# V loads on GpSimd's queue and an earlier trigger for K loads in a batched decode attention kernel

## The chip, the cores and the metric

The kernel runs on 1 core of a Trainium2 chip. The metric is the device time of one execution in microseconds. A profile of one execution goes with each version: its times run from the first to the last instruction (the span). The engines are TensorE (PE), VectorE (DVE), ScalarE (ACT), GpSimd (POOL) and SyncE (SP). Each runs its own instruction stream in order and waits on semaphores; SyncE only issues DMAs here.

## The reference

Eight sequences each decode one token. x is 8 x 1 x 640, and K and V caches are 8 x 32 heads x 4096 keys x 128, all in bf16. The output is the sum of x, an attention block and an MLP block, both on the normalized x:

```python
def _A_ref(x, k_cache, v_cache, wq, wo):
    q = (x @ wq).reshape(B, Sq, Hq, Dh).transpose(0, 2, 1, 3)
    scores = jnp.einsum("bhqd,bhkd->bhqk", q, k) * (Dh ** -0.5)
    p = _softmax(scores, axis=-1)
    o = jnp.einsum("bhqk,bhkd->bhqd", p, v)
    return o.transpose(0, 2, 1, 3).reshape(B, Sq, Hq * Dh) @ wo

def _B_ref(x, w1, b1, w2, b2):
    y = _layernorm(x, axis=-1)
    return _gelu(y @ w1 + b1) @ w2 + b2

xn = _layernorm(x, axis=-1)
return x + _A_ref(xn, ...) + _B_ref(xn, ...)
```

Every head has its own K and V, read once. They are 537 MB of the 552 MB that the kernel reads.

## The kernel before, in words

The work is cut into NQ = 32 pairs; pair i is one sequence with 8 heads. Its K is one load of 128 partitions x 256 keys x 128 (8.389 MB, 64 KB per partition), its V another of the same size. On chip there are three slots of that size: KA for the K of even pairs, KB for that of odd pairs, and VS for every V. So K(i) can be loaded once the K of pair i-2 is used up, and V(i) once the V of pair i-1 is.

A pair goes through these steps, named as in the code:

- `qrep(i)` (GpSimd) repeats the pair's queries, `pe_qbc(i)` and `act_qbc(i)` (TensorE, ScalarE) spread them over the partitions into `qbc_sb`.
- `k_ready(i)` (GpSimd) waits for K(i) and sets a small tile, on which TensorE's work of the pair waits.
- The scores of 80 of the 256 keys in each partition are made on TensorE: `pe_T` turns K tiles (transposes, the last of them is `kt`), `act_T` copies them from PSUM, `pe_QK` multiplies. Those of the other 176 keys are made on VectorE in three chunks (`dve_chunk`: multiply by `qbc_sb`, add halves, reduce); the end of the last chunk is `km`. `dve_sel` brings TensorE's scores in before the third chunk.
- `dve_max(i)` makes the maximum (`nb`), and `act_exp(i)` takes the exps of 8 heads; it waits for `nb` of its pair and for the PV of the pair before, since P_sb has one buffer.
- `pe_PV(i)` multiplies the 256 blocks of V by the exps, once V(i) and the exps are there; `act_O` copies the result out, and `o_norm` (GpSimd) scales it.

TensorE runs the scores of pair i+1 before PV(i). After the last pair come the MLP and the output projection with wo; their weights are loaded into slots that have come free (w1 and w2 into KA after pair 30, wo into KB after pair 31). V(30) is loaded in two parts.

The order on each engine is fixed by hand: each step is entered with a position, all are sorted by it, and each engine replays its calls in that order. With o = 100 i: `load_k(i)` stands at o - 51, `qrep(i)` at o - 52, `act_qbc(i)` at o - 10.5, `k_ready(i)` at o - 2, `load_v(i)` at o + 50, `act_exp(i)` at o + 90, `pe_PV(i)` at o + 150, `act_O(i)` at o + 171, `o_norm(i)` at o + 175. A waiting instruction holds up all that follows on its engine. In the kernel before, SyncE issues all K and V loads, in turn, and all land in one hardware queue. `KLATE = 6`: the first K loads wait for `kt` and `km` of pair i-2, those from pair 6 on for its exps. All operations are recorded through one helper, so the profile shows line 111 for nearly all of them.

Of the kernel before, what the change touches and what calls it, by code (L numbers as in the profile page):

```python
# [192 lines left out]
def bass_parallel_sum__gqa_block_cached__mixer_channel_mlp__decode_kernel(  # L193
# [34 lines left out]
    TPB = 8  # L228
    NS = 2
    LOOP0, LOOPN = 2, 15  # L230
    KLATE = 6
    assert NKEY == 256 and NQ == 32
    SLOT = NKEY * DH
    KA, KB, VS = 0, 1, 2
# [4 lines left out]
    V_CUT = (0, 192, 256)  # L239
# [4 lines left out]
    def chunks(i):  # L244
        jd = NKEY - jp_of(i)
        n = 3
        return [(jd * c // n, jd * (c + 1) // n) for c in range(n)]

    def kslot(i):
        return KA if i % 2 == 0 else KB  # L250
# [8 lines left out]
    with ExitStack() as es:  # L259
        sb = lambda name, shape, dt: es.enter_context(nc.sbuf_tensor(name, shape, dt))  # L260
        ps = lambda name, shape, dt: es.enter_context(nc.psum_tensor(name, shape, dt))
        sem = lambda name: es.enter_context(nc.semaphore(name))

        S_sb = sb("S_sb", [P, 3, SLOT], BF)
        tile = [S_sb[:, s, :].rearrange("p (j d) -> p j d", d=DH) for s in range(3)]
# [6 lines left out]
        def scratch(n, rows=P, slot=KB):  # L272
# [71 lines left out]
        pe, dve, act, sp, pool = (_Eng(sem(f"{n}_s")) for n in ("pe", "dve", "act", "sp", "pool"))  # L344
        pe2, act2, fin, fin2 = (_Eng(sem(n)) for n in ("pe2_s", "act2_s", "fin_s", "fin2_s"))
        ld_s = [_Dma(sem(f"ld_s{s}")) for s in range(3)]
        ld_x, ld_b1, ld_b2, ld_wq, ld_w1, ld_w2a, ld_w2b, st_a, st_o = (
            _Dma(sem(n)) for n in ("ld_x", "ld_b1", "ld_b2", "ld_wq", "ld_w1", "ld_w2a", "ld_w2b", "st_a", "st_o"))
        ld_vl = [_Dma(sem(f"ld_vl{q}")) for q in range(1, len(V_CUT) - 1)]
        ld_wl = [_Dma(sem(f"ld_wl{q}")) for q in range(2)]  # L350
        ld_wn = [_Dma(sem(f"ld_wn{q}")) for q in range(len(WN_CUT) - 1)]
        tk = {}
# [8 lines left out]
        def cache_src(cache, i):  # L361
            hq, b = divmod(i, B)
            return cache[b, hq * HS:(hq + 1) * HS].rearrange("h (p j) d -> (h p) j d", j=NKEY)

        def load_k(i):
            s = kslot(i)
            if i >= KLATE:
                sp.wait(tk[("exp", i - 2)])
            elif i >= 2:
                sp.wait(tk[("kt", i - 2)], tk[("km", i - 2)])  # L370
            elif s == KB:
                sp.wait(tk["qmm"])
            tk[("k", i)] = ld_s[s].sig(sp.dma_start(tile[s], cache_src(A_k_cache, i)))
# [4 lines left out]
            load("w2a", ld_w2a, w2_sb, B_w2[0:FB * P, :].rearrange("(p c) n -> p c n", c=FB))  # L378

        def load_v(i):  # L380
            sp.wait(tk["qmm"] if i == 0 else tk[("pv", i - 1)])
            if i != NQ - 2:
                tk[("v", i)] = [ld_s[VS].sig(sp.dma_start(tile[VS], cache_src(A_v_cache, i)))]
                return
            tk[("v", i)] = []
            for d, lo, hi in zip([ld_s[VS]] + ld_vl, V_CUT[:-1], V_CUT[1:]):
                if lo:
                    d.n += 1
                tk[("v", i)].append(
                    d.sig(sp.dma_start(tile[VS][:, lo:hi, :], cache_src(A_v_cache, i)[:, lo:hi, :])))  # L390

        def load_b1():
            act.wait(tk[("kt", NQ - 2)], tk[("km", NQ - 2)])
# [226 lines left out]
        def dve_chunk(i, c):  # L620
            s = i % 2
            lo, hi = chunks(i)[c]
            w = hi - lo
            kt = tile[kslot(i)][:, lo:hi, :]
            dve.wait(tk[("k", i)], tk[("qb", i)])
            t = dve.sig(dve.tensor_tensor(
                kt, kt, qbc_sb[:, s, :][:, None, :].to_broadcast([P, w, DH]), ALU.mult))
            tk[("ym", i)] = t
            dve.wait(t)
            t = dve.sig(dve.tensor_tensor(kt[:, :, 0:DH // 2], kt[:, :, 0:DH // 2], kt[:, :, DH // 2:DH], ALU.add))  # L630
            dve.wait(t, tk.get(("exp", i - 2)))
            tk[("km", i)] = dve.sig(dve.tensor_reduce(Sd_sb[:, s, lo:hi], kt[:, :, 0:DH // 2], AX.X, ALU.add))
# [179 lines left out]
        at(NQ * Q - 55, load_mlp)  # L812
        at(NQ * Q - 54.9, load_w2b)
        at(-870, load_k, 0)
        at(NQ * Q - 60.1, zero_w2b)
        at(-800, consts_pool)
# [17 lines left out]
        for i in range(NQ):  # L834
            o = i * Q
            last = i == NQ - 1
            if i:
                at(o - 51, load_k, i)
            at(o + 50, load_v, i)
            at(o - 52, qrep, i)  # L840
            at(o - 2, k_ready, i)
            at(o - 11, pe_qbc, i)
            at(o - 10.5, act_qbc, i)
            nt = jp_of(i) // TPB
            w = 42.0 / nt
            for t in range(nt):
                at(o + w * t, pe_T, i, t)
                at(o + w * (t + 0.4), act_T, i, t)
                at(o + w * (t + 1.5), pe_QK, i, t)
            at(o + 2, dve_chunk, i, 0)  # L850
            at(o + 26, dve_chunk, i, 1)
            at(o + 52, dve_sel, i, 0)
            at(o + 55, dve_sel, i, 1)
            at(o + 58, dve_chunk, i, 2)
            at(o + 84, dve_max, i)
            at(o + 90 if i else o + Q + 45, act_exp, i)
            at(o + Q + 48, pe_RS, i)
            at(o + Q + 57, dve_rinv, i)
            at(o + Q + 50, pe_PV, i)
            if not last:  # L860
                at(o + Q + 71, act_O, i)
            at(o + Q + 75, o_norm, i)
# [81 lines left out]
```

## Time and profile before

| | |
|---|---|
| time, median of 3 runs | 1281.4 us (1281.25 to 1281.62) |
| span of the profiled execution | 1280.1 us |
| read from HBM | 551.80 MB, 431 GB/s over the span |
| share of the 16 DMA engines' time in SyncE's queue | 99.7% |
| VectorE busy | 1101.6 us, 86% |
| TensorE busy | 672.0 us, 52% |
| ScalarE busy | 477.0 us, 37% |
| GpSimd busy | 109.3 us, 9% |
| mean granted TensorE clock | 0.564 |

The rows of the timeline give a start, a duration, an engine, the operation with its output and inputs, and in brackets how long the engine had stood idle and what ended that. "SPq" and "ACTq" are DMA issues: they show when a load was handed to a queue, not when it moved. In the list of issues the last number is the median time from issue to landing.

### The profile page before, as it was taken

Reading aid. Unit: us, or ns where it says so; the run is one execution under the profiler, and the core shown is the slowest. Engines: PE = TensorE matmul, PEld = TensorE weight load, DVE = VectorE, ACT = ScalarE, POOL = GpSimd, SP = SyncE. Lnnn points to the kernel's source line nnn. Section 1 sums busy time; section 2 is a strip of 40 time slices with the busy share of each in tenths; the row PEclk is TensorE's granted clock in tenths of the full one; section 3 lists DMA queues with packets and bytes.
Section 4 is the critical chain, followed back from the end, with each engine's and each line's share of the span. In section 5 each row is a group of like instructions: output and inputs, shape, how many; then the busy total and the mean of one; then the engine's idle time right before and its main releaser. Section 6 shows DMA issues by size and latency. Waiting matters only on the chain.

```text
span 1280.1 us, 34355 instructions
## 1 busy us (share of the span) xinstructions
PE 672.0 (52%) x13906; PEld 573.2 (45%) x13906; DVE 1101.6 (86%) x681; ACT 477.0 (37%) x906; POOL 109.3 (9%) x119
## 2 busy tenths in 40 slices
PE   1636555446645446545456554456454466464476
PEld 1435444335535345444345444345343355353465
DVE  1899999889888889888898888898888898888894
ACT  0524444233444233443234443234442334442331
POOL 0020010000000000000000000000000000000050
PEclk9755565565565556555555555556555656655665
DMA  9999999999999999999999999999999999999998
GB/s 419 427 433 431 432 430 432 442 432 430 430 442 428 432 432 436 436 430 432 432 442 430 430 432 438 432 430 434 436 436 430 432 430 442 432 428 434 432 440 367
DMA packets 10785, 551.99 MB, mean 431 GB/s; under 512 B 1242, under 2 KB 1523, under 8 KB 1812
## 3 DMA queue, kind: packets, MB, share of 16 engines
q1 hardware_dynamic: 10736, 551.79, 99.7%
q8 instruction: 9, 0.15, 0.0%
q10 hardware_dynamic: 36, 0.02, 0.0%
q14 instruction: 4, 0.03, 0.0%
HBM read 551.80 MB, written 0.01 MB: 431 GB/s over the span
## 4 chain that ended last, share of the span: by engine, by line
DMA 47%; DVE 37%; issue 11%; ACT 4%; DVEq 0%; SPq 0%; PE 0%
DMA S_sb<-in_A_k_cache_dram 45%; DVE S_sb L111 26%; DVE Sd_sb L111 8%; ACT P_sb L111 4%; DMA S_sb<-in_A_wo_dram 2%; DVE S_ps L111 1%; DVE mx_sb L111 1%; DVE mbT_sb L111 0%; DVE mxT_sb L111 0%; DVE ri_sb L111 0%; DVE NB_sb L111 0%; DVEq L109 0%; DVE mq_sb L111 0%; DVE mb_sb L111 0%; SPq L111 0%
## 5 line engine op out<-in xcount | busy, mean ns | idle before, releaser
L111 PE MATMUL TR_ps<-ident_bf,S_sb 128*128 128x128 bf16 (+1 forms) x2570 | 343.3, 280 | 353.5 <-POOL kr_sb L111 333.2
L111 DVE TENSOR_TENSOR S_sb<-S_sb,qbc_sb 128x7552 bf16<-128x7552 bf16 (+1 forms) x96 | 388.7, 4049 | 128.3 <-DMA S_sb<-in_A_k_cache_dram 128.0
L111 PEld LDWEIGHTS TR_ps<-ident_bf,S_sb 128*128 (+2 forms) x2570 | 245.7, 103 | 411.7 <-issue 338.5
L111 DVE TENSOR_REDUCE Sd_sb<-S_sb 128x59 f32<-128x3776 bf16 (+1 forms) x96 | 390.2, 4065 | 6.0
L111 ACT ACTIVATE KT_sb<-TR_ps 128x1024 bf16<-128x1024 bf16 x320 | 327.0, 1024 | 121.6 <-PE TR_ps L111 109.6
L111 PE MATMUL PV_ps<-P_sb,S_sb 128*128 128x8 bf16 x8192 | 224.0, 175 | 140.6 <-DMA S_sb<-in_A_v_cache_dram 137.9
L111 PEld LDWEIGHTS PV_ps<-P_sb,S_sb 128*128 128x128 bf16 x8192 | 221.3, 103 | 143.3 <-DMA S_sb<-in_A_v_cache_dram 140.5
L111 DVE TENSOR_TENSOR S_sb<-S_sb 128x3776 bf16<-128x3776 bf16 (+1 forms) x96 | 206.5, 2151 | 3.3
L111 ACT ACTIVATE P_sb<-Sd_sb,NB_sb 128x256 bf16<-128x256 f32 x256 | 126.3, 494 | 210.9 <-DVE NB_sb L111 210.9
L111 PE MATMUL S_ps<-qrep_sb,KT_sb 128*128 128x8 bf16 x2560 | 121.9, 177 | 50.9 <-ACT KT_sb L111 47.8
L111 ACT ACTIVATE oU_sb<-PV_ps 128x8 f32<-128x8 f32 x31 | 5.5, 178 | 375.8 <-PE PV_ps L111 375.8
L111 PEld LDWEIGHTS S_ps<-qrep_sb,KT_sb 128*128 128x128 bf16 x2560 | 91.7, 103 | 82.4 <-ACT KT_sb L111 41.1
L111 POOL TENSOR_TENSOR oT_sb<-oU_sb,ri_sb 128x8 bf16<-128x8 f32 x31 | 71.8, 2315 | 370.8 <-DVE S_sb L111 315.3
L111 POOL COPY qrep_sb<-qT_sb 128x128 bf16<-128x128 bf16 x32 | 18.3, 573 | 474.7 <-PE S_ps L111 455.1
L111 ACT ACTIVATION_READ_ACCUMULATOR P_sb<-Sd_sb,NB_sb 128x1 f32 x256 | 47.8, 187 | 0.0
L111 DVE TENSOR_TENSOR S_ps<-S_ps,mask_sb 128x320 f32<-128x320 f32 (+1 forms) x65 | 31.6, 486 | 2.7 <-PE S_ps L111 2.7
L111 DVE TENSOR_REDUCE Sd_sb<-S_ps 128x40 f32<-128x320 f32 x64 | 31.5, 492 | 2.2
L111 PE MATMUL QB_ps<-ident_bf,qrep_sb 128*128 128x128 bf16 x32 | 9.1, 285 | 40.7 <-DVE S_sb L111 22.1
L111 ACT ACTIVATE qbc_sb<-QB_ps 128x128 bf16<-128x128 f32 x32 | 8.9, 278 | 57.6 <-PE QB_ps L111 57.6
L111 POOL MEMSET kr_sb<- 128x1 f32 x32 | 3.2, 99 | 294.9 <-DMA S_sb<-in_A_k_cache_dram 294.9
L111 PEld LDWEIGHTS QB_ps<-ident_bf,qrep_sb 128*128 128x128 bf16 x32 | 3.3, 103 | 43.6 <-ACT oU_sb L111 29.0
L111 PE MATMUL CH_ps<-rs_sb,ones_f 128*128 128x8 f32 x64 | 15.4, 313 | 6.5 <-ACT P_sb L111 6.5
(68 smaller groups left out, 150.6 us busy)
## 6 DMA issues: line engine op xcount, KB each, us to landing
S_sb<-in_A_v_cache_dram SPq DMA_DIRECT2D x1, 6144.0 KB, 26.8
S_sb<-in_A_wq_dram SPq DMA_DIRECT2D x1, 5120.0 KB, 15.6
S_sb<-in_A_wo_dram SPq DMA_DIRECT2D x1, 2560.0 KB, 18.4
S_sb<-in_B_w_dram SPq DMA_DIRECT2D x1, 2160.0 KB, 30.3
S_sb<-in_B_w_dram SPq DMA_DIRECT2D x1, 2080.0 KB, 34.9
S_sb<-in_A_v_cache_dram SPq DMA_DIRECT2D x1, 2048.0 KB, 31.4
S_sb<-in_A_wo_dram SPq DMA_DIRECT2D x1, 1280.0 KB, 21.1
S_sb<-in_A_wo_dram SPq DMA_DIRECT2D x1, 800.0 KB, 22.6
```

The source lines that it names most:

```text
L111: inst = getattr(e, name)(*a, **k)
```

## The change

V loads are issued by GpSimd, and so go into a queue of their own, with a semaphore `ld_g` of their own. V(0) waits, beside the last use of wq (`qmm`), for a multiply of pair 0's second chunk (`ym0`). The second part of V(30) stays on SyncE, which waits for the same PV. K loads stay on SyncE; all of them now wait for `kt` and `km` of pair i-2, and none for its exps.

```diff
-    KLATE = 6
...
+        ld_g = _Dma(sem("ld_g"))
...
         def load_k(i):
             s = kslot(i)
-            if i >= KLATE:
-                sp.wait(tk[("exp", i - 2)])
-            elif i >= 2:
+            if i >= 2:
                 sp.wait(tk[("kt", i - 2)], tk[("km", i - 2)])
             elif s == KB:
                 sp.wait(tk["qmm"])
...
         def load_v(i):
-            sp.wait(tk["qmm"] if i == 0 else tk[("pv", i - 1)])
+            pool.wait(*([tk["qmm"], tk["ym0"]] if i == 0 else [tk[("pv", i - 1)]]))
             if i != NQ - 2:
-                tk[("v", i)] = [ld_s[VS].sig(sp.dma_start(tile[VS], cache_src(A_v_cache, i)))]
+                tk[("v", i)] = [ld_g.sig(pool.dma_start(tile[VS], cache_src(A_v_cache, i)))]
                 return
             tk[("v", i)] = []
-            for d, lo, hi in zip([ld_s[VS]] + ld_vl, V_CUT[:-1], V_CUT[1:]):
+            for d, lo, hi in zip([ld_g] + ld_vl, V_CUT[:-1], V_CUT[1:]):
                 if lo:
                     d.n += 1
+                    sp.wait(tk[("pv", i - 1)])
                 tk[("v", i)].append(
-                    d.sig(sp.dma_start(tile[VS][:, lo:hi, :], cache_src(A_v_cache, i)[:, lo:hi, :])))
+                    d.sig((sp if lo else pool).dma_start(
+                        tile[VS][:, lo:hi, :], cache_src(A_v_cache, i)[:, lo:hi, :])))
...
             tk[("ym", i)] = t
+            if i == 0 and c == 1:
+                tk["ym0"] = t
```

## The prediction

> **What bounds the kernel now.** I read the page's first parts for the balance of the engines, then the issues with their landing times, then two neighbouring pairs in the timeline.
>
> ```profile
> PE 672.0 (52%) x13906; PEld 573.2 (45%) x13906; DVE 1101.6 (86%) x681; ACT 477.0 (37%) x906; POOL 109.3 (9%) x119
> ...
> q1 hardware_dynamic: 10736, 551.79, 99.7%
> ...
> HBM read 551.80 MB, written 0.01 MB: 431 GB/s over the span
> ```
>
> SyncE's queue q1 carries all but 0.02 MB and keeps the 16 DMA engines busy for 99.7% of the span. VectorE, next at 86%, has slack. The bytes don't change, so the possible gain is small: 0.3% of 1281.4 us is 3.8 us. The question is whether the wire stays full.
>
> ```profile
> S_sb<-in_A_k_cache_dram SPq DMA_DIRECT2D x32, 38.7
> S_sb<-in_A_v_cache_dram SPq DMA_DIRECT2D x31, 31.6
> ...
> 391.67 0.33 SPq L111 DMA_DIRECT2D S_sb<-in_A_v_cache_dram  x1
> 403.89 0.33 SPq L111 DMA_DIRECT2D S_sb<-in_A_k_cache_dram  x1
> 430.36 0.33 SPq L111 DMA_DIRECT2D S_sb<-in_A_v_cache_dram  x1
> 442.60 0.33 SPq L111 DMA_DIRECT2D S_sb<-in_A_k_cache_dram  x1
> ```
>
> One pair takes 442.60 − 403.89 = 38.71 us. A K and a V load are 8.389 MB each, so the wire moves 16.78 MB in 38.71 us, 433.5 GB/s, and one load alone takes 19.35 us. The queue is first in, first out: a V is issued 12.2 us before a K, so V waits 12.2 us for the rest of the K ahead and then moves in 19.35 us, which is its 31.6 us; K waits for that V and moves: 38.7 us. K and V pass whole and in turn, and there is always one waiting.
>
> Now the chain around them. Call the pair that starts at 404.06 pair i.
>
> ```profile
> 392.78 0.28 ACT L111 ACTIVATE qbc_sb<-QB_ps 128x128 bf16<-128x128 f32 x1 [0.93 <-PE QB_ps L111]
> ...
> 404.06 4.02 DVE L111 TENSOR_TENSOR S_sb<-S_sb,qbc_sb 128x7424 bf16<-128x7424 bf16 x1 [4.27 <-DMA S_sb<-in_A_k_cache_dram]
> ...
> 417.61 0.39 PE L111 MATMUL S_ps<-qrep_sb,KT_sb 128*128 128x8 bf16 x8 [0.81 <-ACT KT_sb L111]
> ...
> 423.34 7.00 PE L111 MATMUL PV_ps<-P_sb,S_sb 128*128 128x8 bf16 x256 [4.91 <-DMA S_sb<-in_A_v_cache_dram]
> ...
> 436.89 0.42 DVE L111 TENSOR_REDUCE mx_sb<-Sd_sb 128x1 f32<-128x256 f32 x1
> ...
> 442.75 4.03 DVE L111 TENSOR_TENSOR S_sb<-S_sb,qbc_sb 128x7424 bf16<-128x7424 bf16 x1 [4.25 <-DMA S_sb<-in_A_k_cache_dram]
> ```
>
> VectorE starts pair i when its K lands and waited 4.27 us for it. Its last chunk is done (`km`) just before 436.89, 32.8 us after its start. The V issue at 391.67 marks the end of PV(i−2), that at 430.36 the end of PV(i−1). The row at 392.78 is `act_qbc(i)`: TensorE and ScalarE do it in program order after PV(i−2) and `act_O(i−2)`, and VectorE cannot start pair i without it. It ends at 393.06, 1.39 us after PV(i−2). Today that is 11.0 us early (404.06 − 393.06), so V has 11.0 us of slack before VectorE feels it.
>
> **The change part by part.** *K's wait.* From pair 6 on, K(i+2) is issued after `km(i)` and `kt(i)` and no longer after `exp(i)`: at 436.9 instead of 442.60, 5.7 us earlier. (`kt(i)` is older: the last scores of pair i run at 417.61.) On a wire that is full this gains nothing; it only makes the K queue start earlier.
>
> *V's queue.* V's trigger is the same, the end of PV(i−1). GpSimd has ahead of it `k_ready(i)` and `qrep(i+1)`, which want K(i) landed and the last scores of pair i. TensorE does those scores before PV(i−1) anyway, so they delay nothing. Behind the waiting load stand `o_norm(i−1)`, which needs PV(i−1) too, and `k_ready(i+1)`, which lets TensorE begin pair i+1; that has the exps in between to spare. What GpSimd itself does can be slow beside VectorE:
>
> ```profile
> 70.10 4.02 DVE L111 TENSOR_TENSOR S_sb<-S_sb,qbc_sb 128x7424 bf16<-128x7424 bf16 x1
> 70.11 4.17 POOL L111 COPY qrep_sb<-qT_sb 128x128 bf16<-128x128 bf16 x1 [14.51 <-PE S_ps L111]
> ```
>
> That copy ended with VectorE's multiply. No row shows a load issued by GpSimd. I bound its issue by SyncE's 0.33 us and by this 4.17 us; near 0.33, because at the end of a PV VectorE will be idle (below). Either way a K is on the wire meanwhile, so its cost is 0.
>
> *Two queues on one wire.* This is the step that decides. With one queue V waits for the K ahead and then has the wire alone. With two, does it share? The only pair of queues in the trace is at the end, where ScalarE loads b1 (3.4 KB) past SyncE's backlog:
>
> ```profile
> S_sb<-in_B_w_dram SPq DMA_DIRECT2D x1, 2080.0 KB, 34.9
> ...
> S_sb<-in_B_b_dram ACTq DMA_DIRECT2D x1, 3.4 KB
> ...
> 1211.00 12.53 SPq L111 DMA_DIRECT2D S_sb<-in_B_w_dram  x10
> ...
> 1238.48 0.24 ACTq L111 DMA_DIRECT2D S_sb<-in_B_b_dram  x1
> ...
> 1243.22 0.44 PE L111 MATMUL TR_ps<-xT_sb,S_sb 128*128 128x8 bf16 x5 [4.92 <-issue]
> ```
>
> The 2080 KB load, issued just after 1211, lands 34.9 us later, at about 1246, and a V stands behind it. The MLP's first matmul at 1243.22 needs b1, so b1 had landed within 4.7 us of its issue, in the midst of that load. Queues are therefore served in turns, in pieces smaller than a load. I take equal halves.
>
> A K is outstanding at every moment (38.7 us in flight, one issued per 38.7 us). So V at half rate takes 2 × 19.35 = 38.7 us instead of 31.6. V, PV and V again then make 38.7 + 7.0 = 45.7 us, against 38.7 for K: V slips by 7 us per pair, and its 11.0 us of slack are gone after two pairs. From then on `act_qbc(i)` is what VectorE waits for, and K(i+2), gated by VectorE, comes late. The loop is then, from the end of PV(i−2):
>
> - 1.39 us to the end of `act_qbc(i)`;
> - 32.8 us of VectorE on pair i (436.89 − 404.06), K(i) long landed; K(i+2) is issued;
> - L, the delay of a load from issue to first data and from last data to the waiting engine;
> - 38.7 us in which K(i+2) and V(i) both pass. V(i) is issued at the end of PV(i−1), some 7 us after K(i+2), and at equal shares it is last. The wire is busy throughout, however the two share it, as long as V ends last;
> - 7.0 us of PV(i) (430.36 − 423.34).
>
> These are two pairs: 79.9 + L. L has two rows:
>
> ```profile
> 0.74 0.40 SPq L111 DMA_DIRECT2D S_sb<-in_A_wq_dram  x1
> 0.75 0.58 ACTq L111 DMA_DIRECT2D S_sb<-in_A_x_dram  x1
> 2.51 0.87 DVE L111 BATCH_NORM_STATS2 S_sb<-S_sb 8x6 f32<-8x320 bf16 x2 [0.35 <-DMA S_sb<-in_A_x_dram]
> ...
> 16.43 4.43 PE L111 MATMUL CH_ps<-xT_sb,S_sb 128*128 128x8 bf16 x160 [8.01 <-DMA S_sb<-in_A_wq_dram]
> ```
>
> The tiny x load takes 2.51 − 0.75 = 1.8 us, nearly all L. wq's 5.243 MB need 12.1 us at 433.5 GB/s and take 15.7: L = 3.6. I take 2.6, the middle: a load is large as wq is, but not the first of the program. So (79.9 + 2.6) / 2 = 41.3 us per pair, 2.6 more than 38.7; with the two ends of L 40.9 and 41.8. In each pair the wire stands idle for these 2.6 us, between a V's landing and the next K.
>
> *The sum.* Before pair 5 V only uses up slack, and the wire is full. From there to V29's landing I count 25 such gaps: 25 × 2.6 = 65 us. Then comes one longer gap. While PV(29) runs, K31 has landed, V30 waits for PV(29), and the MLP weights wait for VectorE's pair 30: 7.0 + 2.6 = 9.6 us. After that V30, the weights, V31 and wo keep the wire full, in whatever order.
>
> ```profile
> 1204.45 0.80 SPq L111 DMA_DIRECT2D S_sb<-in_A_v_cache_dram  x2
> ...
> 1265.62 7.00 PE L111 MATMUL PV_ps<-P_sb,S_sb 128*128 128x8 bf16 x256 [5.92 <-DMA S_sb<-in_A_v_cache_dram]
> ...
> 1277.57 0.65 PE L111 MATMUL ACC_ps<-S_sb,oS_sb 128*8 128x160 bf16 x12 [0.26 <-DMA S_sb<-in_A_wo_dram]
> ```
>
> V31 will share with wo and land later, but today PV(31) ends at 1272.6 (1265.62 + 7.00) and the last matmuls still wait for wo's last piece, to 1277.57: that is 4.9 us of margin. I take the end's own cost at 0; if V31 came in last of all, it would cost those 7.0 us of PV less the margin, 2 us. Splitting V30 over two queues is free: its second part is needed only after pair 31's scores. Together 65 + 9.6 = 75 us. The profiled span of 1280.1 becomes 1355; the median, 1.3 us above the span, becomes 1281.4 + 75 = 1356 us. With L's ends the loss is 25 × 2.2 + 8.8 = 64 and 25 × 3.1 + 10.6 = 88: this case's own range is 1345 to 1369.
>
> **The rivals.** *V does not slip* (no slower). V keeps up if issue to landing stays below 38.7 − 7.0 = 31.7 us. That holds if queues take turns by whole loads, since V then waits 12.2 us and moves in 19.35 as now, or if V gets two thirds of the wire or more (19.35 × 1.5 + 1.8 = 30.8). The rhythm of today stays: 1281, less at most the 3.8 us that the wire leaves. Against it stands b1, which did not wait for the load it met to end. [...]
>
> *K gets more than half.* The loop stays 82.5 us for two pairs, as V is last all the more, but V is behind from the start and the lag is not made good at the end: up to one V load more, 75 + 19 = 94 us, 1375; if even and odd pairs fall unevenly, up to another such load more.
>
> *Faster.* The wire's 0.3% and the tail could give at most 3.8 us: 1278.
>
> **How the numbers follow.** Forecast 0.68, on b1's row and the loop; V does not slip 0.15; K gets more 0.14; faster 0.03. From 1300 to 1395 the range takes in the forecast, shares between it and the first rival, and the second rival, and leaves out the first and the gain, 0.18 in all. A measurement of this kernel can tell about 0.2%, 2.6 us, from no change: faster by more 0.04, within 0.09 (most of the first rival), slower 0.87.
>
> **What would show it.** Right: the DMA share falls from 99.7% to about 94%; V's landing time rises above 31.6 us, toward 34; K issues come 41.3 us apart; VectorE's waits name QB_ps/`qbc_sb` where they named K's DMA, and its share falls to about 81%; TensorE waits about 16 us for V before each PV instead of 4.9. Wrong: VectorE still waits for K's DMA by about 4 us per pair and the wire stays at 99%, then V did not slip; or V's landing time far above 40 us, then K has the larger share; or a period of 41 with the wire full, then the rate fell.

## The result, and the profile after

The changed kernel takes 1368.1 us (1366.8 to 1369.0, four runs) against 1281.5 us: a ratio of 1.0675, 95% interval 1.0662 to 1.0687. The forecast was 1356, range 1300 to 1395. The profiled executions have spans of 1367.4 and 1280.1 us, 87.3 apart.

From the first parts of the page after: the engines' shares, the two queues, and what was read.

```profile
PE 669.9 (49%) x13906; PEld 571.9 (42%) x13906; DVE 1104.6 (81%) x681; ACT 467.3 (34%) x906; POOL 58.8 (4%) x151
...
q1 hardware_dynamic: 6128, 285.45, 49.7%
q0 software_dynamic: 4608, 266.34, 45.2%
...
HBM read 551.80 MB, written 0.01 MB: 404 GB/s over the span
```

TensorE, VectorE and ScalarE run the instructions they did (13906, 681 and 906); GpSimd has 32 more, its V loads. The two queues together fill 94.9% of the DMA engines' time where one filled 99.7%. That share counts the time that transfers took, and they took longer: 94.9% of 1367.4 us is 1298 us, 99.7% of 1280.1 is 1276, for the same bytes. So some 21 of the 87 us lie in longer transfers and the other 66 in DMA engines without work. By the single DMA records of the trace, most of the longer ones are first pieces of a K load: of 397 pieces of 64 KB in K's queue that took over 15% more than the usual 2.42 us, 392 began within 3 us of a K's issue (in the kernel before, 11 pieces of 64 KB took that long). Now the waits (total, times, longest) of before:

```profile
PE PV_ps L111 <- DMA S_sb<-in_A_v_cache_dram: 137.9, 29, 5.9
DVE S_sb L111 <- DMA S_sb<-in_A_k_cache_dram: 128.0, 28, 14.5
```

and of after:

```profile
PE PV_ps L111 <- DMA S_sb<-in_A_v_cache_dram: 483.0, 32, 18.8
DVE S_sb L111 <- ACT qbc_sb L111: 195.0, 29, 9.5
DVE S_sb L111 <- DMA S_sb<-in_A_k_cache_dram: 15.1, 1, 15.1
```

The list of issues of after (the last number is the median from issue to landing):

```profile
S_sb<-in_A_k_cache_dram SPq DMA_DIRECT2D x32, 34.0
S_sb<-in_A_v_cache_dram POOLq DMA_DIRECT2D x31, 34.2
```

VectorE no longer waits for K (but for the first) but for the spread query, 29 times; TensorE waits for V three and a half times as long; V's flight, its time from issue to landing, has grown from 31.6 to 34.2 us. The timeline of after shows the loop of two pairs:

```profile
711.76 7.00 PE L111 MATMUL PV_ps<-P_sb,S_sb 128*128 128x8 bf16 x256 [16.84 <-DMA S_sb<-in_A_v_cache_dram]
719.06 0.57 POOL L111 DMA_DIRECT2D S_sb<-in_A_v_cache_dram  x1 [24.17 <-PE PV_ps L111]
719.95 0.28 ACT L111 ACTIVATE qbc_sb<-QB_ps 128x128 bf16<-128x128 f32 x1 [0.97 <-PE QB_ps L111]
...
720.26 4.03 DVE L111 TENSOR_TENSOR S_sb<-S_sb,qbc_sb 128x7424 bf16<-128x7424 bf16 x1 [7.53 <-ACT qbc_sb L111]
...
753.08 0.42 DVE L111 TENSOR_REDUCE mx_sb<-Sd_sb 128x1 f32<-128x256 f32 x1
759.61 0.57 POOL L111 DMA_DIRECT2D S_sb<-in_A_v_cache_dram  x1 [22.75 <-PE PV_ps L111]
...
794.38 7.00 PE L111 MATMUL PV_ps<-P_sb,S_sb 128*128 128x8 bf16 x256 [17.31 <-DMA S_sb<-in_A_v_cache_dram]
801.68 0.57 POOL L111 DMA_DIRECT2D S_sb<-in_A_v_cache_dram  x1 [24.30 <-PE PV_ps L111]
```

PV(i-2) ends at 718.76. The query is spread 1.47 us later and VectorE starts pair i at once. It is done at 753.08, 32.8 us on, and K(i+2) can go out. V(i), issued at 759.61, is there at 794.38, 41.3 us after K(i+2) was let go, and PV(i) takes 7.0. From V issue to V issue but one: 801.68 - 719.06 = 82.62 us, 41.31 per pair.

Where the 87 us lie can be read from the wire, since the bytes are the same. Windows of before, then of after, cut at V issues; the last column is GB/s:

```profile
0.00:100.00 100.00, 39.47 (x770) 33.20 (x770) 68.83 (x57) 28.39 (x45) 11.06 (x20) 0.74 0.99 425
100.00:198.16 98.16, 59.06 (x1248) 50.70 (x1248) 96.17 (x59) 43.06 (x82) 6.72 (x7) 0.55 1.00 434
198.16:1165.75 967.59, 507.29 (x10475) 432.21 (x10475) 848.35 (x501) 368.38 (x700) 67.58 (x75) 0.55 1.00 433
...
1204.45:1280.10 75.65, 45.92 (x995) 39.89 (x995) 54.41 (x47) 22.43 (x51) 21.13 (x14) 0.57 0.95 406
```

```profile
0.00:100.00 100.00, 36.99 (x760) 31.02 (x760) 68.74 (x57) 27.78 (x44) 10.62 (x22) 0.75 0.99 420
100.00:223.34 123.34, 61.22 (x1257) 52.31 (x1257) 105.86 (x67) 43.32 (x84) 2.94 (x9) 0.51 0.96 409
223.34:1255.12 1031.78, 507.36 (x10475) 431.81 (x10475) 846.64 (x500) 359.85 (x700) 30.21 (x100) 0.55 0.95 406
1255.12:1297.03 41.91, 20.34 (x419) 17.34 (x419) 33.87 (x20) 14.40 (x28) 1.24 (x5) 0.54 0.78 339
1297.03:1367.40 70.37, 43.96 (x995) 39.40 (x995) 49.47 (x38) 21.91 (x50) 13.81 (x16) 0.55 0.90 376
```

A window loses its length times (1 - rate / 433.5). The 25 pairs in the middle lose 1031.78 x (1 - 406 / 433.5) = 65.5 us and nothing before; the window of PV(29) loses 9.1; the start up to PV(3) loses 7.0 plus 1.2 more than before; the end loses 9.3 where it lost 4.8. That is 87.3.

### The profile page after: what moved, and what is told of

Same layout as the page of the kernel before. It is cut to its first block, busy times and chain, and to the rows that moved or that the text cites. A ratio compares the mean times of both kernels' runs of the same rounds, so it can differ in the third digit from the quotient of the medians.

```text
span 1367.4 us, 34381 instructions
## 1 busy us (share of the span) xinstructions
PE 669.9 (49%) x13906; PEld 571.9 (42%) x13906; DVE 1104.6 (81%) x681; ACT 467.3 (34%) x906; POOL 58.8 (4%) x151
## 3 DMA queue, kind: packets, MB, share of 16 engines
q0 software_dynamic: 4608, 266.34, 45.2%
## 4 chain that ended last, share of the span: by engine, by line
DMA 39%; issue 29%; PE 19%; ACT 6%; DVE 5%; POOL 1%; SPq 0%; POOLq 0%
DMA S_sb<-in_A_v_cache_dram 37%; PE TR_ps L111 8%; PE PV_ps L111 8%; ACT P_sb L111 4%; PE S_ps L111 3%; DVE S_sb L111 3%; DMA S_sb<-in_A_k_cache_dram 3%; ACT KT_sb L111 2%; DVE Sd_sb L111 2%; POOL S_sb L111 1%; POOL qrep_sb L111 0%; PE QB_ps L111 0%; PE ACC_ps L111 0%; ACT oU_sb L111 0%; DVE S_ps L111 0%
## 5 line engine op out<-in xcount | busy, mean ns | idle before, releaser
L111 DVE TENSOR_TENSOR S_sb<-S_sb,qbc_sb 128x7552 bf16<-128x7552 bf16 (+1 forms) x96 | 395.2, 4116 | 210.1 <-ACT qbc_sb L111 195.0
L111 PE MATMUL PV_ps<-P_sb,S_sb 128*128 128x8 bf16 x8192 | 224.0, 175 | 485.6 <-DMA S_sb<-in_A_v_cache_dram 483.0
L111 ACT ACTIVATE KT_sb<-TR_ps 128x1024 bf16<-128x1024 bf16 x320 | 323.2, 1021 | 81.7 <-PE TR_ps L111 72.8
L111 DVE TENSOR_TENSOR S_sb<-S_sb 128x3776 bf16<-128x3776 bf16 (+1 forms) x96 | 202.9, 2114 | 3.3
L111 POOL DMA_DIRECT2D S_sb<-in_A_v_cache_dram x32 | 18.4, 574 | 712.1 <-PE PV_ps L111 711.9
L111 POOL COPY qrep_sb<-qT_sb 128x128 bf16<-128x128 bf16 x32 | 15.0, 468 | 536.9 <-PE S_ps L111 517.6
L111 DVE TENSOR_TENSOR S_ps<-S_ps,mask_sb 128x320 f32<-128x320 f32 (+1 forms) x65 | 31.6, 486 | 2.7 <-PE S_ps L111 2.7
L111 PEld LDWEIGHTS QB_ps<-ident_bf,qrep_sb 128*128 128x128 bf16 x32 | 3.3, 103 | 44.4 <-ACT oU_sb L111 27.1
L111 PEld LDWEIGHTS CH_ps<-rs_sb,ones_f 128*128 128x128 f32 x64 | 13.5, 263 | 5.7 <-DVE S_sb L111 3.7
## 6 DMA issues: line engine op xcount, KB each, us to landing
S_sb<-in_A_wq_dram SPq DMA_DIRECT2D x1, 5120.0 KB, 15.2
```

The source lines that it names most:

```text
L111: inst = getattr(e, name)(*a, **k)
```

## The experiments

Times are medians; the kernel before stood at 1281.5 to 1281.7 us beside them. "Period" is the mean distance of the 26 steps from PV(3)'s end to PV(29)'s: 38.70 us before, 41.30 after. Since V(i+1) is issued when PV(i) ends, the period is V's flight, plus the wait of a PV after it, plus 7.0 us.

**The two halves of the change.** `k_only` is the kernel before with the change's wait for K. `v_only` is the changed kernel with K's old wait:

```diff
# k_only, on the kernel before
-            if i >= KLATE:
-                sp.wait(tk[("exp", i - 2)])
-            elif i >= 2:
+            if i >= 2:
# v_only, on the changed kernel
+            if i >= 6:
+                sp.wait(tk[("exp", i - 2)])
-            if i >= 2:
+            elif i >= 2:
```

> Only the K part of the change: V stays on SyncE, K waits for scores and km. Theory (two queues share the wire piece by piece, V slips, act_qbc holds VectorE, K comes late): one queue, so no sharing; K still follows V in order and the wire is full: 1279 to 1284 us, DMA share 99%, K issues 38.7 us apart. Rival 1 (K issued 5.7 us earlier pushes V back by itself): most of the 87 us, 1340 or more. Rival 2 (the earlier trigger is worth something once the queues are left alone): below 1278.

> Only the V part: V on GpSimd's queue, K from pair 6 on waits for the exps as before. Theory: exp(i) waits for PV(i-1), and V(i) is issued at the same PV's end, so K(i+2) and V(i) start within 6 us of each other and share from the start: V takes about 3.4 + 2 x 16 = 35 us, plus about 4 us of delays and 7 us of PV: 46 to 49 us per pair, 1480 to 1560 us, much slower than the whole change. The earlier K trigger is then what limits the damage. Rival 1 (the earlier K trigger does the harm): back to 1281. Rival 2 (only the queue matters, the trigger not): 1368.

`k_only`: 1281.5 us, ratio 0.9999 (0.9989 to 1.0009), period 38.70. `v_only`: 1439.8 us, 1.1236 (1.1217 to 1.1255), period 44.04. The issues of `k_only`, then V's of `v_only`:

```profile
S_sb<-in_A_k_cache_dram SPq DMA_DIRECT2D x32, 44.4
S_sb<-in_A_v_cache_dram SPq DMA_DIRECT2D x31, 31.6
```

```profile
S_sb<-in_A_v_cache_dram POOLq DMA_DIRECT2D x31, 36.7
```

In one queue K merely waits 5.7 us longer (44.4 against 38.7) and lands no sooner. So the whole loss is V's queue, and the earlier K makes it smaller. Why, the timeline of `v_only` shows:

```profile
783.90 0.42 DVE L111 TENSOR_REDUCE mx_sb<-Sd_sb 128x1 f32<-128x256 f32 x1
...
793.89 0.57 POOL L111 DMA_DIRECT2D S_sb<-in_A_v_cache_dram  x1 [26.21 <-PE PV_ps L111]
...
794.95 0.50 ACT L111 ACTIVATE P_sb<-Sd_sb,NB_sb 128x256 bf16<-128x256 f32 x1
...
799.01 0.33 SPq L111 DMA_DIRECT2D S_sb<-in_A_k_cache_dram  x1
```

VectorE is done with the scores of pair i at 783.90, but the exps must wait for PV(i-1), which ends at 793.6. So K(i+2) goes out 15.1 us after the scores, not 5.7 as in the kernel before. V(i) and K(i+2) both start from the end of the same PV, K 5.1 us after V, and the loop is one of a single pair: 0.3 us to V's issue, 36.7 of flight and 7.0 of PV are 44.0, the period. That is the expectation's mechanism; its time was too high because it put V's flight with its delays at 39 us.

**Who issues V.** `v_act` has ScalarE issue V, at o + 71.5, in a hardware queue:

```diff
-            pool.wait(*([tk["qmm"], tk["ym0"]] if i == 0 else [tk[("pv", i - 1)]]))
+            act.wait(*([tk["qmm"], tk["ym0"]] if i == 0 else [tk[("pv", i - 1)]]))
...
-                tk[("v", i)] = [ld_g.sig(pool.dma_start(tile[VS], cache_src(A_v_cache, i)))]
+                tk[("v", i)] = [ld_g.sig(act.dma_start(tile[VS], cache_src(A_v_cache, i)))]
...
-            at(o + 50, load_v, i)
+            at(o + 71.5, load_v, i)
...
```

> As the change, but V is issued by ScalarE right after act_O, in ScalarE's hardware queue; ScalarE's stream is written out instead of looped, since each load has its own address. Theory (any second queue shares the wire): 1350 to 1370 us, K issues 40.5 to 41.5 us apart, VectorE waits for qbc_sb. Rival (it is GpSimd's way of issuing loads that is slow or late): 1281 to 1290.

1380.2 us, 1.0765 (1.0747 to 1.0783); period 41.32. From its issues, then from the timeline of its end:

```profile
S_sb<-in_A_v_cache_dram ACTq DMA_DIRECT2D x31, 34.2
```

```profile
1323.68 0.33 ACTq L111 DMA_DIRECT2D S_sb<-in_A_v_cache_dram  x1
1324.05 0.31 ACTq L111 DMA_DIRECT2D S_sb<-in_B_b_dram  x1
...
1351.21 0.44 PE L111 MATMUL TR_ps<-xT_sb,S_sb 128*128 128x8 bf16 x5 [27.57 <-issue]
```

VectorE waits 192.6 us in all for `qbc_sb` (195.0 in the changed kernel). Flight, wait and period are those of GpSimd's queue: the second queue costs, not the engine that issues. The 12 us above the changed kernel, for which the expected 1350 to 1370 was missed, lie after the issue of V(31), at 1323.7 us against 1328.4 in the changed kernel. Here b1, which ScalarE loads for the MLP, is issued behind V(31) into ScalarE's own queue (4644 records on the page, 36 in the changed kernel). With the 25.6 us that V(31) takes in the changed kernel, it would land at about 1349.3, by estimate; the MLP starts at 1351.2, 27.2 us after b1's issue, the exps of pair 31 follow the MLP on ScalarE, and PV(31) starts at 1365.3. In the changed kernel no V is in ScalarE's queue, the MLP starts 1.7 us after b1's issue, and PV(31) at 1354.1, when V(31) lands. So this end seems to come from what shares a queue with what, and not from ScalarE's issue of loads; no run moves b1 alone.

**The size of the pieces.** A load moves as 128 pieces, one per partition (the 4608 records of queue q0 are 32 loads of 128 pieces and 16 records of 4 bytes each). `k_half` and `k_quart` cut each K load by keys into 2 and 4 loads (32 and 16 KB per partition), `v_half` cuts each V load in two.

```diff
-            tk[("k", i)] = ld_s[s].sig(sp.dma_start(tile[s], cache_src(A_k_cache, i)))
+            for c in range(2):      # k_quart: 4
+                lo, hi = NKEY * c // 2, NKEY * (c + 1) // 2
+                tk[("k", i)] = ld_s[s].sig(sp.dma_start(tile[s][:, lo:hi, :], cache_src(A_k_cache, i)[:, lo:hi, :]))
# v_half
-                tk[("v", i)] = [ld_g.sig(pool.dma_start(tile[VS], cache_src(A_v_cache, i)))]
+                for lo in (0, NKEY // 2):
+                    tk[("v", i)] = [ld_g.sig(pool.dma_start(
+                        tile[VS][:, lo:lo + NKEY // 2, :], cache_src(A_v_cache, i)[:, lo:lo + NKEY // 2, :]))]
...                             # the first part of V(30) is cut in two as well
```

> The change with each K load in two loads of 32 KB per partition, same trigger, same bytes. Theory (the wire's engines change queue after every piece of one row): K's pieces are half as large, V gets two thirds of the wire and needs about 29 us and 3 of delays, which is at the 31.7 us where V stops slipping: 1281 to 1325 us, V issue to landing 30 to 33 us. Rival 1 (equal time to each queue, whatever the pieces): 1368, V 34 us. Rival 2 (queues change by whole loads): 1368 or worse.

> The change with each V load in two loads of 32 KB per partition. Theory (an engine changes queue after every piece): V gets one third while K is on the wire and ends last in each stretch, as before, so the two-pair loop has the same length: period 41.3 us, and some more at the start: 1368 to 1395. If pairs fall unevenly, so that a K ends before the next V begins, more. Rival 1 (more V pieces in flight help V): below 1360. Rival 2 (V's landing time sets the period directly: 38.7 x 1.25 and more): 1500 and more.

> The changed kernel with each K load in four DMAs of 64 keys (16 KB per partition). Theory: the two queues take turns piece by piece, one partition row each, so what a queue gets is set by the size of its pieces. V's 64 KB against K's 16 KB gives V about four fifths while both are there: 19.35 x 1.25 = 24.2 us, with K's late and V's late ends some 28 us from issue to landing, under the 31.7 us from which V slips. Then the rhythm of before comes back: 38.7 to 39.2 us per pair, DMA share over 98%, and 1281 to 1300 us. Rival, the size of the pieces has done what it can with halves, and what is left of the loss is the order of the work (PV, then the query for VectorE): V's landing stays near the 33.1 us of halves and the time within 1320 to 1340.

`k_half`: 1333.2 us, 1.0409 (1.0391 to 1.0426), period 40.47. `v_half`: 1384.0, 1.0798 (1.0780 to 1.0816), period 41.36. `k_quart`: 1344.7, 1.0484 (1.0467 to 1.0502), period 40.81. The issues of the three, in this order:

```profile
S_sb<-in_A_k_cache_dram SPq DMA_DIRECT2D x64, 4096.0 KB, 33.1
S_sb<-in_A_v_cache_dram POOLq DMA_DIRECT2D x31, 33.1
```

```profile
S_sb<-in_A_v_cache_dram POOLq DMA_DIRECT2D x62, 4096.0 KB, 27.8
S_sb<-in_A_k_cache_dram SPq DMA_DIRECT2D x32, 27.9
```

```profile
S_sb<-in_A_k_cache_dram SPq DMA_DIRECT2D x128, 2048.0 KB, 25.0
S_sb<-in_A_v_cache_dram POOLq DMA_DIRECT2D x31, 27.3
```

Two waits of `k_quart`:

```profile
PE PV_ps L111 <- DMA S_sb<-in_A_v_cache_dram: 11.1, 4, 9.8
DVE S_sb L111 <- DMA S_sb<-in_A_k_cache_dram: 186.6, 12, 18.5
```

V's flight goes from 34.2 to 33.1 to 27.3 us as K's pieces shrink, and K's from 34.0 to 27.9 as V's do: the smaller piece loses. The single DMA records of the changed kernel's trace say the same. They name no engine, but laid end to end they make 16 rows, and in each row K and V alternate, one piece each, while both are there (from 762 to 785 us in the changed kernel, for one), 2.42 us for 64 KB. Near that kernel's end the pieces differ, and still they alternate but for one pair of neighbours: from 1302 to 1320 us V(30)'s of 48 KB (1.82 us) with SyncE's of 16 KB (0.61 us). The shares follow the size of the pieces.

The time is another matter. In `k_half` V is still above the 31.7 us of the prediction's threshold, and the loss falls from 87 to 52 us; both numbers lie just above what its theory expected (to 33 us and to 1325), and both rivals (1368) are out. In `k_quart` V is well below it and TensorE hardly waits for V. But now K is late: VectorE waits for K's DMA in every third pair, and V goes out unevenly. V issues in the timeline of `k_quart`:

```profile
621.00 0.57 POOL L111 DMA_DIRECT2D S_sb<-in_A_v_cache_dram  x1 [7.10 <-PE PV_ps L111]
657.79 0.57 POOL L111 DMA_DIRECT2D S_sb<-in_A_v_cache_dram  x1 [7.20 <-PE PV_ps L111]
...
692.52 0.57 POOL L111 DMA_DIRECT2D S_sb<-in_A_v_cache_dram  x1 [7.42 <-PE PV_ps L111]
...
742.53 0.57 POOL L111 DMA_DIRECT2D S_sb<-in_A_v_cache_dram  x1 [6.83 <-PE PV_ps L111]
```

Steps of 36.8, 34.7 and 50.0 us: a third outcome that neither theory had (1281 to 1300, and 1320 to 1340). The wire moves 406 GB/s in the long step and 410 in the one after it, so now it seems to be K's lateness that leaves it short of work; this is read from the waits, and no run takes K's lateness away. `v_half` lands where its theory put it: K's larger share leaves the loop at 41.36, V being last anyway. Of the 15.2 us by which its span (1382.6) exceeds the changed kernel's, the 26 steps hold 1.6 and the two ends the other 14.

**The loop's first link.** `qbc_early` spreads the query for pair i ahead of PV(i-2); `qbc_early_k_half` does that with K in halves.

```diff
-            at(o - 52, qrep, i)
+            at(o - 55 if i else o - 52, qrep, i)
...
-            at(o - 11, pe_qbc, i)
-            at(o - 10.5, act_qbc, i)
+            at(o - 54 if i else o - 11, pe_qbc, i)
+            at(o - 53.5 if i else o - 10.5, act_qbc, i)
...
```

> The change with one link of the loop taken out: qrep, pe_qbc and act_qbc of pair i go before PV(i-2) in program order instead of behind it (one idle repeat for a pair 32 keeps the loops regular), loads and queues as in the change. Theory: VectorE can start pair i without PV(i-2); what then ties it to PV(i-2) is exp(i-1), the scores of pair i and dve_sel: about 0.3 + 4.1 + 12.5 + 1.3 + 10.4 = 28.6 us to km instead of 34.2. The two-pair loop shrinks by 4 to 5.6 us, the period from 41.3 to 38.7 to 39.4, the time to 1285 to 1335. Rival (two queues simply move fewer bytes per us, or GpSimd's loads are late): no gain, 1360 to 1370.

> qbc_early and K in two halves together. Theory: two thirds for V and the shorter chain: the wire is full, period 38.7, 1280 to 1292. Not below 1278, which is what the bytes allow. Rival (a second queue costs rate by itself): 1300 or more.

`qbc_early`: 1319.9 us, 1.0298 (1.0281 to 1.0315), period 39.23. `qbc_early_k_half`: 1316.5, 1.0267 (1.0250 to 1.0284), period 39.86. The issues of the first, V's of the second, then the wait for V in the first:

```profile
S_sb<-in_A_k_cache_dram SPq DMA_DIRECT2D x32, 31.5
S_sb<-in_A_v_cache_dram POOLq DMA_DIRECT2D x31, 32.5
```

```profile
S_sb<-in_A_v_cache_dram POOLq DMA_DIRECT2D x31, 32.9
```

```profile
PE PV_ps L111 <- DMA S_sb<-in_A_v_cache_dram: 435.0, 32, 21.9
```

VectorE waits for `qbc_sb` no more in either, and the period drops by 2.07 us, 54 us over 26 steps: the query after PV was the link that held the changed kernel at 41.3. In `qbc_early`, whose time and period lie where its theory put them, TensorE still waits for V before every PV, and V's flight and PV make 32.5 + 7.0 = 39.5; why V stays in flight that long is not tested. Its windows lose 17 us in the middle (426 GB/s at a DMA share of 0.99, so longer transfers are a good part of it), 8 in the window of PV(29) (342 GB/s), and at the end 8 more than before (358 GB/s over the last 74 us): V still comes to the end behind K. The halves on top took 3 us where I expected some 30, and these at the start: PV(3) ends at 207.0 us instead of 222.9, while the period grew. V's flight did not shorten (32.9), and I had taken V's share while both are there for its share over its whole flight. The rival's time came true here, but its cause only in part: the two queues are busy for 97.9% of 1317.4 us, 1290 us against 1276 before, so 14 of the 37 us are longer transfers and the rest is a wire without work.

**Late K and small K pieces.** `v_only_k_half` has both edits, K's old wait and K in halves, shown above.

> v_only (V on GpSimd, K waits for the exps) with each K load in two loads of 32 KB per partition. Theory: V is issued first and has the wire alone for about 5 us, then gets two thirds: 1.6 + 4.8 + 6 pieces of 3.6 + 0.9 = 29 us, below the 31.7 us where V slips; so V is no longer last, PV ends early, and the wire stays full as with one queue: 1281 to 1295, against 1440 with whole K loads. Rival (the trigger on the exps costs what v_only lost, whatever the pieces): 1400 or more.

1289.4 us, 1.0082 (1.0048 to 1.0116), period 39.12 in the profiled execution, whose span is 1297.7; its ten runs lie from 1287.4 to 1306.5, wider than any other kernel here. V's issues, a wait, and the queues of its page:

```profile
S_sb<-in_A_v_cache_dram POOLq DMA_DIRECT2D x31, 31.7
```

```profile
DVE S_sb L111 <- DMA S_sb<-in_A_k_cache_dram: 140.6, 29, 15.1
```

```profile
q1 hardware_dynamic: 10736, 285.45, 51.1%
q0 software_dynamic: 4608, 266.34, 48.1%
```

The time is in the expected range, V's flight is not: 31.7 us, at the threshold, where 29 was expected. VectorE waits for K as in the kernel before, and the wire is 99.2% full; but 99.2% of 1297.7 us is 1287 us of transfers where the kernel before needed 1276, so 11 of the 17.6 us by which this span is longer lie in longer transfers. The later K cost 72 us with whole loads (1439.8 against 1368.1) and gains 44 with halves (1289.4 against 1333.2). With the old trigger each K goes out some 5 us after a V (V at 793.89 us, K at 799.01 in the rows of `v_only`), so V is that much ahead. With whole K loads V is late all the same (36.7 us in flight), and the exps and K's request with it, as in `v_only`. With halves V is just in time (31.7 us). These four runs show no more than that; no run moves the trigger in smaller steps.

**The first V.** `v0_early` issues V(0) right after the queries' matmuls, at 20.8 us instead of 50.5.

```diff
-            pool.wait(*([tk["qmm"], tk["ym0"]] if i == 0 else [tk[("pv", i - 1)]]))
+            pool.wait(tk["qmm"] if i == 0 else tk[("pv", i - 1)])
...
-            at(o + 50, load_v, i)
+            at(o + 50 if i else o - 53, load_v, i)
```

> The changed kernel with V of pair 0 issued by GpSimd as soon as the queries' matmuls are done, some 29 us earlier (it was issued at 50.5 us, behind the copy for pair 1; SyncE issued it at 21.3 us before the change). Theory, the loop of two pairs sets the time and V slips against K in the first pairs whatever its start: the first PVs come up to 6 us earlier, the period stays 41.3, and the time is 1362 to 1368 us. Rival, the late first V is what made the first four pairs 25 us later: 1343 to 1350 us.

1379.9 us, 1.0765 (1.0747 to 1.0783), period 41.28. VectorE's one wait for K, at pair 0:

```profile
DVE S_sb L111 <- DMA S_sb<-in_A_k_cache_dram: 26.5, 1, 26.5
```

It was 15.1 us in the changed kernel: V(0) now shares the wire with K(0), K(0) lands 11.4 us later, and all the rest with it (the span is 10.4 us longer). Both theories missed that, so the cost of the late first V was not isolated. The period stayed.

## Why the prediction was right, and where its sizes were off

- *The wire is full, an earlier K gains nothing.* Shown by `k_only`: 0.9999.
- *Two queues share the wire in pieces.* Shown by the flights of the three cut kernels. That the shares were equal stood on no row (b1 showed turns only) and was an assumption; it held because both loads have pieces of 64 KB, which alternate one each in the DMA records. Turns by whole loads, as in the first rival, would by its sum (12.2 + 19.35) have left V its 31.6 us. It took 34.2, and 27.3 against quarter pieces.
- *GpSimd's issue costs nothing.* It took 0.57 us, near the lower bound, and `v_act` has the same period (41.32).
- *V's slack is gone after two pairs, then the query binds.* VectorE's wait is on `qbc_sb`, and `qbc_early`, which moves only the steps of that link, brings the period from 41.30 to 39.23. Shown.
- *The loop: 79.9 + L, 41.3 us per pair.* Measured 82.62 for two pairs in the rows above; so L comes to 2.7 where 2.6 was taken. The DMA share of 94% (94.9), V's landing toward 34 (34.2), VectorE's 81% and TensorE's wait before each PV (16 us forecast, 483.0 / 32 = 15.1) came nearly as written.
- *25 gaps, 65 us, and one of 9.6.* Measured 65.5 and 9.1. These are losses by rate. The prediction called them an idle wire; in part they are the longer first pieces of K.
- *What was mis-sized: the two ends, at zero.* "Before pair 5 V only uses up slack, and the wire is full": the start lost 7.0 + 1.2 us. VectorE's first long wait for the query, 9.47 us, comes at 182.98 us, already in pair 4. The prediction took the steady slack of 11.0 us and a V flight of 38.7 us as valid from the first pair. But V(0), behind GpSimd's copy, goes out at 50.5 us where it went at 21.3, and V(2) is in flight for 42 us (issued at 132.37, its PV starts at 174.49). Which of the two weighs more is open, since `v0_early` disturbed K(0). "I take the end's own cost at 0", bound 2: it was 4.5. Together these are the 12 us between 1356 and 1368. That the case's own range, to 1369, held them is luck: it was made from the two ends of L, and L was right.
- *K gets more than half.* `v_half` brings it about: period unchanged, the ends 14 us longer, where the rival had up to 19.

## What to carry to other kernels

Where a full wire feeds two streams, one queue can act as a schedule: here K, issued 5.7 us earlier, landed no sooner (`k_only`, 44.4 us against 38.7), and V kept its 31.6 us. With a second queue the two streams shared the wire by the size of the pieces (V's flight 34.2, 33.1 and 27.3 us against K pieces of 64, 32 and 16 KB), and V, which has a single buffer, put its longer flight straight into the period (34.2 + 7.0 us, 41.30 measured); before splitting, compare flight plus use with the period. An earlier request can help or harm by turns, as K's did here (72 us one way, 44 the other), so trigger and piece size have to be tried together.

## What was not expected of the hardware

The unit of a turn was one piece, in the changed kernel's DMA records at 64 against 64 KB and at 48 against 16 KB alike: cutting K's loads to a quarter took V's flight from 34.2 to 27.3 us and made K the late one. And no kernel with two queues came back to one queue's time: the best stood at 1.0082 (1.0048 to 1.0116), with the wire 99.2% full by time but with longer transfers, and its runs spread over 19 us where those of the kernel before lie within 2.
